# Rounding the low weight bits on ScalarE, fewer fill matmuls, and a later start of the scheduled loop

## The chip, the cores and the metric

The kernel runs on one core of one Trainium2 chip. The metric is the device time of one execution in microseconds, from a set of runs on the chip; beside it stands one execution that the hardware profiler recorded. A core has five engines, and each runs its own queue of instructions in order: PE (TensorE, matmuls), DVE (VectorE), ACT (ScalarE), POOL (GpSimd) and SP (SyncE, which here issues all DMAs). They wait for each other through semaphores.

## The reference

Three stages. An attention with a running state over 8 heads of 40, 768 tokens and a batch of 2; a first expert stage; a second one. Cut to what matters:

```python
m_new  = max(f + m, i);  f_s = exp(f + m - m_new);  i_s = exp(i - m_new)
C = f_s * C + i_s * outer(v, k);  n = f_s * n + i_s * k
y = sigmoid(o) * (C @ q) / max(|n . q|, 1)             # per head and token

h = max(x @ w1, x @ w2, x @ w3);  x = h @ w_out        # 320 -> 768 -> 320
h = x @ w_in;  g = h * tanh(log1p(exp(h)));  out = g @ w_out2   # 320 -> 2048 -> 320
```

The weights reach the chip as 64-bit floats, each as two 32-bit integer words (low, high).

## The kernel before, in words

**Tiles and stages.** Tokens come in 12 units of 128 (6 chunks of the sequence times 2 batches); blocks of 512 tokens (4 units) are what the expert stages work on. The matmuls run at a precision that takes each operand apart into a rounded high part and the rest (`xh` and `xl`, `w` with both, `hh` and `hl`), so one product is eight matmuls of 512 columns (`mm8`, line 340: five with `xh`, three with `xl`).

**A unit** runs through `spread` (line 139, tile `fp`: the decays on PE), `decay` (line 124, tile `dt`: two scans on DVE), `scores` (line 162, tiles `sc_0` and `sc_1`: keys times queries on PE, even heads from rows 0 to 63, odd heads from rows 64 to 127), `passed` (line 150, `cp`), `decayed` (line 167: `dt` times scores on DVE), `values` and `keys` on POOL (lines 173 and 184, `vp` and `kp`), `numer` (lines 204 and 206, tile `it`), `denom` (lines 212 to 214 on DVE, then line 216 `sg` times 1/den on POOL), `gated` (line 221 on DVE, tile `xn`; line 222 its pad on ACT), `transpose_x` (line 233 on PE, tile `xp`; line 235 the copy to `xh` on ACT), `lower_x` (`xl`), `outer` (line 256, `sp`) and `carry` (lines 268 and 270, the state `st`).

**A weight** is a tile of 128 x 640 numbers. `fetch` loads the raw words (`raw`, three buffers). `scaled` (line 285, ACT) takes the high word as a float times a power of two into `dec`. `merge` is three passes on DVE: line 292 shifts the low word right by 29 and sets its last bit (`low`), line 294 shifts `dec` left by 3 and ORs `low`, line 296 puts the sign bit back into `dec`. Then ACT (lines 307 to 309) rounds to the high part and POOL (lines 310 to 312) subtracts. There are 28 weights: nine `w` of the first expert stage, three plus eight `wo`, eight `wi`.

**What sets the order.** Lines 392 to 547 are one hand-written order on all engines: the setup, units 0 to 3 and the first product (`up(0, 0)`). In it `dummy` puts fill matmuls on PE whose result nobody reads (line 193, 128 x 512 from the tile `warm`, a part of `zraw`). The rest, from `follow(PLAN0)` on, gets its order from a scheduler at build time, which may put the loop's instructions between the hand-written ones once the last of some of them have gone out: line 581 names the five, on PE the `fence`, which is the last matmul of `outer(3)`. PLAN0 is `w2 a4 w3 u0.1 a5 w4 b4 w5 w6 b5 a6 w7 w8 a7 u0.2 b6 ...` (w a weight, a `attend`, b `finish`, u `up`).

Of the kernel before, what the change touches and what calls it, by code (L numbers as in the profile page):

```python
# [10 lines left out]
AF = mybir.ActivationFunctionType  # L11
ALU = mybir.AluOpType
PSUM = bass.MemoryType.PSUM

P = 128
B, H, S, D = 2, 8, 768, 40
# [20 lines left out]
BLOCKS = ((0, 512), (512, 512), (1024, 256), (1280, 256))  # L37
NU = NC * B
I32 = mybir.dt.int32


@with_exitstack
def mlstm_moe_kernel(ctx, tc, fi0, fir, qk2, q3, nat, w13, wo1, wi2, wo2, ident, bmask, out):
    nc = tc.nc
# [3 lines left out]
    stage = ctx.enter_context(tc.tile_pool(name="stage", bufs=1))  # L48
# [14 lines left out]
    def bank(tag, name):  # L63
        if tag == "mm":
            return mmp.tile([P, 512], F32, tag=tag, name=name)
        return pat.tile([P, 512], F32, tag=tag, bufs=3 if tag == "sm" else 1, name=name)
# [4 lines left out]
    idt = ac.tile([P, P + 2 * BH + 1], F32, tag="idt", name="idt")  # L71
# [42 lines left out]
    unit = {u: {} for u in range(NU)}  # L114
    warm = zraw[:, 0, 0:256].bitcast(mybir.dt.bfloat16)

    def heads(ap, e):
        return ap.rearrange("p (h e) -> p h e", h=H)
# [46 lines left out]
    def decayed(u, j):  # L165
        t = unit[u]
        nc.vector.tensor_tensor(t["dt"][:, j::2], t["sc"][j].rearrange("p (h t) -> p h t", h=4), t["dt"][:, j::2], op=ALU.mult)
# [18 lines left out]
    def gateo(u):  # L186
        sg = a2.tile([P, H, D], F32, tag="sg", name=f"sg{u}")
        nc.scalar.activation(sg, heads(loads[u][1][:, H * VD + DM:], D), AF.Sigmoid)
        unit[u]["sg"] = sg

    def dummy(ps, n):
        for _ in range(n):
            nc.tensor.matmul(ps, warm[:, 0:P], warm, start=True, stop=True)

    def numer(u, ps=None):
        c, b = u // B, u % B
        t = unit[u]
        ps = itbank(f"it{u}") if ps is None else ps
        it = heads(ps[:, 0:H * VD], VD)
        vt = vps[u % 2]  # L200
        for g in range(3):
            h1 = min(3 * g + 3, H)
            if c > 0:
                nc.tensor.matmul(it[:, 3 * g:h1], t["cb"][:, g], st[b][:, 3 * g:h1], start=True, stop=False)  # L204
            for h in range(3 * g, h1):
                nc.tensor.matmul(it[:, h], t["dt"][:, h], vt[:, h], start=(c == 0), stop=(c == 0 or h == h1 - 1))  # L206
        t["it"] = it

    def denom(u):
        num = unit[u]["it"]  # L210
        den = a2.tile([P, H, 1], F32, tag="den", name=f"den{u}")
        nc.vector.tensor_scalar(den, num[:, :, D:VD], -1.0, 1.0, op0=ALU.mult, op1=ALU.max)
        nc.vector.tensor_tensor(den, den, num[:, :, D:VD], op=ALU.max)
        nc.vector.reciprocal(den, den)
        sg = unit[u]["sg"]
        nc.gpsimd.tensor_tensor(sg, sg, den.to_broadcast([P, H, D]), op=ALU.mult)

    def gated(u):
        t = unit[u]
        xn = a2.tile([P, 3 * P], F32, tag="xn", name=f"xn{u}")  # L220
        nc.vector.tensor_tensor(heads(xn[:, 0:DM], D), t["it"][:, :, 0:D], t["sg"], op=ALU.mult)
        nc.scalar.activation(xn[:, DM:3 * P], xn[:, 2 * P:DM], AF.Copy)
        t["xn"] = xn

    def transpose_x(u, xp=None, fill=0):
        xh, xl = xs[u // 4]
        col = u % 4 * L
        xn = unit[u]["xn"]
        xp = bank("sm", f"xp{u}") if xp is None else xp
        dummy(xp, fill)  # L230
        xp = xp[:, 0:3 * L].rearrange("p (j t) -> p j t", j=3)
        for j in range(3):
            nc.tensor.transpose(xp[:, j], xn[:, j * P:(j + 1) * P], idt[:, 0:P])
        unit[u]["xp"] = xp
        return nc.scalar.activation(xh[:, :, col:col + L], xp, AF.Copy)  # L235

    def lower_x(u):
        xh, xl = xs[u // 4]
        col = u % 4 * L
        if u < B:  # L240
            xr = m1.tile([P, 3, L], F32, tag=f"hl{4 + u}", bufs=1, name=f"xr{u}")
            nc.scalar.activation(xr, unit[u]["xp"], AF.Copy)
            return lambda: nc.gpsimd.tensor_tensor(xl[:, :, col:col + L], xr, xh[:, :, col:col + L].bitcast(F32), op=ALU.subtract)
        if u >= 4:
            xr = a2.tile([P, 3, L], F32, tag="xr", bufs=1, name=f"xr{u}")
            nc.scalar.activation(xr, unit[u]["xp"], AF.Copy)
            return nc.gpsimd.tensor_tensor(xl[:, :, col:col + L], xr, xh[:, :, col:col + L].bitcast(F32), op=ALU.subtract)
        return nc.vector.tensor_tensor(xl[:, :, col:col + L], unit[u]["xp"], xh[:, :, col:col + L].bitcast(F32), op=ALU.subtract)

    def outer(u, sp=None, fill=0):  # L250
        sp = bank("sm", f"sp{u}") if sp is None else sp
        dummy(sp, fill)
        sp = sp[0:120, 0:9 * VD].rearrange("p (h e) -> p h e", h=9)
        kt, vt = kps[u % 2], vps[u % 2]
        for g in range(3):
            pe = nc.tensor.matmul(sp[:, 3 * g:3 * g + 3], kt[:, 3 * g:3 * g + 3].rearrange("p h e -> p (h e)"), vt[:, 3 * g:3 * g + 3], start=True, stop=True)  # L256
        unit[u]["sp"] = sp
        return pe
# [13 lines left out]
    raws = {}  # L272

    def fetch(src, name):
        raw = stage.tile([P, 640, 2], I32, tag="raw", bufs=RB, name=f"raw_{name}")
        raws[name] = raw
        return nc.sync.dma_start(raw, src)
# [3 lines left out]
    def scaled(src, name):  # L281
        if name not in raws:
            fetch(src, name)
        a = stage.tile([P, 640], F32, tag="dec", bufs=2, name=f"dec_{name}")
        nc.scalar.activation(a, raws[name][:, :, 1].bitcast(F32), AF.Copy, scale=2.0 ** -112)
        decs_[name] = a

    def merge(name):
        raw, a = raws.pop(name), decs_[name]
        lo, hi = raw[:, :, 0], raw[:, :, 1]  # L290
        t = stage.tile([P, 640], I32, tag="low", bufs=1, name=f"low_{name}")
        nc.vector.tensor_scalar(t, lo, 29, 1, op0=ALU.logical_shift_right, op1=ALU.bitwise_or)  # L292
        yield
        nc.vector.scalar_tensor_tensor(t, a.bitcast(I32), 3, t, op0=ALU.logical_shift_left, op1=ALU.bitwise_or)
        yield
        nc.vector.scalar_tensor_tensor(a.bitcast(I32), hi, -2147483648, t, op0=ALU.bitwise_and, op1=ALU.bitwise_or)

    def decode(src, name):
        scaled(src, name)
        for _ in merge(name):  # L300
            pass
        return decs_.pop(name)

    def split_lhs(z, w, eng):
        z = z.rearrange("p (s f) -> p s f", f=P)
        t = z[:, 4]
        nc.scalar.activation(w[:, 0:4], z[:, 0:4], AF.Copy)
        nc.scalar.activation(w[0:64, 8], t[0:64], AF.Copy)
        nc.scalar.activation(w[64:128, 9], t[64:128], AF.Copy)
        eng.tensor_tensor(w[:, 4:8], z[:, 0:4], w[:, 0:4].bitcast(F32), op=ALU.subtract)  # L310
        eng.tensor_tensor(w[64:128, 8], t[0:64], w[0:64, 8].bitcast(F32), op=ALU.subtract)
        return eng.tensor_tensor(w[0:64, 9], t[64:128], w[64:128, 9].bitcast(F32), op=ALU.subtract)
# [3 lines left out]
    def load_w13(g):  # L316
        name = f"w13_{g}"
        z = decs_.pop(name) if name in decs_ else decode(w13[g], name)
        w = wpool.tile([P, 10, P], F32R, tag=f"wa{g}", name=name)
        w1t[g] = w  # L320
        return split_lhs(z, w, nc.gpsimd)
# [70 lines left out]
    with tc.manual_schedule(engines={ET.PE, ET.DVE, ET.SP, ET.Activation, ET.Pool}):  # L392
# [7 lines left out]
        f, i = ft0[:, 0], ft0[:, 1]  # L400
# [84 lines left out]
        keys(2)  # L485
        nc.scalar.activation(gTr, gq[:, 0:NR * BH], AF.Copy)
        denom(1)
        carry(1)
        decayed(2, 0)
# [8 lines left out]
        mg = merge("w13_0")  # L498
# [13 lines left out]
        decayed(3, 0)  # L512
        queries(3)
        decayed(3, 1)
        transpose_x(1, bank("mm", "xp1"), 4)
        low1 = lower_x(1)
        denom(2)
        for _ in mg:
            pass
        next(mg, None)  # L520
        gateo(3)
        it3 = bank("sm", "it3")
        dummy(it3, 4)
        numer(3, it3)
        gated(2)
        denom(3)
        low1()
        scaled(w13[1], "w13_1")
        load_w13(0)
        mg = merge("w13_1")  # L530
        next(mg)
        outer(2, bank("mm", "sp2"))
        transpose_x(2, bank("mm", "xp2"), 4)
        next(mg)
        gated(3)
        for _ in mg:
            pass
        fsp = fetch(w13[3], "w13_3")
        fence = outer(3, bank("sm", "sp3"))
        lower_x(2)  # L540
        fact = transpose_x(3, bank("sm", "xp3"), 6)
        fetch(w13[2], "w13_2")
        fdve = lower_x(3)
        fpool = load_w13(1)
# [86 lines left out]
    low = {}  # L631
# [137 lines left out]
```

## Time and profile before

| | us |
|---|---|
| median of 3 runs | 403.36 (403.31 to 403.39) |
| the profiled execution | 404.21 |
| its span, first to last instruction | 402.4 |

The page of the profile gives the busy time of each engine over the span. A list of waits says for what an engine stood idle and how long. A table by window gives, for each stretch of the span, what each engine was busy, how many instructions it ran and which TensorE clock was granted (1.00 is the higher of its two levels, 2.4 GHz; 0.50 the lower, 1.2 GHz). A timeline gives instructions in order of time, runs of like ones in one line. Matmuls overlap their neighbours in these records, so the time of a group is read from its start to the start of what follows.

### The profile page before, as it was taken

What the parts mean: (1) busy time and instruction counts of PE and PEld (TensorE: products, weight loads), DVE (VectorE), ACT (ScalarE), POOL (GpSimd) and SP (SyncE); (2) the same over time, 40 slices, a digit from 0 to 9 for tenths busy, and PEclk for the clock granted to TensorE, in tenths of its full rate; (3) what the DMA queues carried; (4) which work ended last, traced back from release to release, by engine and by line L of the source; (5) the groups of instructions that cost most, each with busy time, mean ns of one, the idle gap of its engine ahead of it and who ended that gap; (6) DMA issues with size and microseconds to landing.
All of it is one profiled execution on the core that took longest, in us unless ns stands there. A gap on an engine that the chain in (4) does not pass through costs nothing.

```text
span 402.4 us, 6169 instructions
## 1 busy us (share of the span) xinstructions
PE 394.7 (98%) x2376; PEld 347.3 (86%) x2376; DVE 216.4 (54%) x340; ACT 173.2 (43%) x389; POOL 154.4 (38%) x155
## 2 busy tenths in 40 slices
PE   8999999999999999999999999999999999999996
PEld 5787887788888888888888889999898999999996
DVE  6897999678927277306823769962211221322220
ACT  3545655533543322256443586553332233434331
POOL 6666768934822223438851446651000010001000
PEclk9999999699999999999999999999999999999999
DMA  7696455632630012002320234300100000100100
GB/s 206 195 305 207 147 186 196 205 106 90 221 109 3 2 65 67 0 2 64 132 68 0 91 107 148 115 0 2 65 0 2 0 2 0 67 0 2 34 0 33
DMA packets 10410, 32.61 MB, mean 81 GB/s; under 512 B 1405, under 2 KB 4285, under 8 KB 10381
## 3 DMA queue, kind: packets, MB, share of 16 engines
q1 hardware_dynamic: 10381, 32.23, 24.8%
q8 instruction: 18, 0.29, 0.3%
q14 instruction: 11, 0.09, 0.1%
HBM read 30.26 MB, written 1.97 MB: 80 GB/s over the span
## 4 chain that ended last, share of the span: by engine, by line
PE 87%; DVE 6%; issue 3%; POOL 2%; ACT 1%; DMA 0%; DVEq 0%; POOLq 0%; ACTq 0%
PE h L340 22%; PE mm L340 21%; PE o L661 7%; PE o L663 7%; PE o L662 7%; PE it L206 4%; PE sc L162 3%; PE mz L371 2%; PE mz L372 2%; PE mz L373 2%; PE fp L139 2%; PE it L204 1%; DVE low_w L292 1%; PE sp L256 1%; DVE dt L124 1%
## 5 line engine op out<-in xcount | busy, mean ns | idle before, releaser
L645 DVE TENSOR_TENSOR gl<-g,gh 128x512 fp32r<-128x512 f32 (+1 forms) x64 | 38.3, 599 | 97.2 <-ACT g L644 97.2
L340 PE MATMUL mm<-xh,w 128*128 128x512 f32 x270 | 74.4, 403 | 0.6 <-ACT xh L235 0.6
L340 PE MATMUL h<-zh,wi 128*128 128x512 f32 (+1 forms) x320 | 67.7, 338 | 0.0
L643 ACT ACTIVATE gh<-h 128x512 fp32r<-128x512 f32 (+1 forms) x64 | 31.4, 491 | 83.6 <-PE h L340 77.6
L340 PEld LDWEIGHTS mm<-xh,w 128*128 128x128 f32 x270 | 50.4, 192 | 11.2 <-ACT xh L235 0.8
L663 PE MATMUL o<-wo,gl 128*128 128x320 f32 x192 | 59.4, 309 | 0.0
L662 PE MATMUL o<-wo,gh 128*128 128x320 f32 x192 | 59.3, 309 | 0.0
L661 PE MATMUL o<-wo,gh 128*128 128x320 f32 x192 | 59.2, 309 | 0.0
L340 PEld LDWEIGHTS h<-zh,wi 128*128 128x128 f32 x320 | 51.4, 189 | 4.7
L614 POOL TENSOR_TENSOR zl<-zraw,zh 128x512 fp32r<-128x512 f32 (+1 forms) x12 | 13.0, 1090 | 91.5 <-ACT zh L613 91.5
L340 PE MATMUL mm<-xl,w 128*128 128x512 f32 x162 | 47.8, 399 | 0.0
L340 PE MATMUL h<-zl,wi 128*128 128x512 f32 (+1 forms) x192 | 44.5, 338 | 0.0
L360 POOL TENSOR_TENSOR hl<-zraw,hh 128x512 fp32r<-128x512 f32 x18 | 25.4, 1411 | 47.6 <-ACT hh L359 47.4
L357 DVE TENSOR_TENSOR zraw<-zraw,mm 128x512 f32<-128x512 f32 x36 | 24.6, 682 | 33.6 <-PE mm L340 33.6
L661 PEld LDWEIGHTS o<-wo,gh 128*128 128x128 f32 x192 | 36.1, 188 | 1.3
L662 PEld LDWEIGHTS o<-wo,gh 128*128 128x128 f32 x192 | 36.1, 188 | 1.2
L340 PEld LDWEIGHTS mm<-xl,w 128*128 128x128 f32 x162 | 30.9, 191 | 6.8 <-issue 0.2
L663 PEld LDWEIGHTS o<-wo,gl 128*128 128x128 f32 x192 | 36.1, 188 | 0.0
L340 PEld LDWEIGHTS h<-zl,wi 128*128 128x128 f32 x192 | 31.8, 188 | 4.1
L644 ACT ACTIVATE g<-h 128x512 f32<-128x512 f32 (+1 forms) x64 | 31.2, 487 | 0.0
L124 DVE TENSOR_TENSOR_SCAN dt<-fp,idr 128x512 f32<-128x512 f32 x24 | 28.3, 1206 | 0.1
L206 PE MATMUL it<-vp,dt 128*128 128x41 f32 x192 | 25.2, 272 | 0.7 <-POOL vp L173 0.7
(138 smaller groups left out, 630.3 us busy)
## 6 DMA issues: line engine op xcount, KB each, us to landing
raw_wo<-in_wo_dram SPq DMA_DIRECT2D x11, 640.0 KB
na<-in_nat_dram SPq DMA_DIRECT2D x12, 484.0 KB
raw_w<-in_w_dram SPq DMA_DIRECT2D x9, 640.0 KB
raw_wi<-in_wi_dram SPq DMA_DIRECT2D x8, 640.0 KB
qall<-in_qk_dram SPq DMA_DIRECT2D x24, 160.0 KB
out_dram<-ob SPq DMA_DIRECT2D x12, 160.0 KB
q<-in_q_dram SPq DMA_DIRECT2D x10, 180.0 KB
idt<-in_ident_dram SPq DMA_DIRECT2D x1, 80.5 KB
```

Source lines behind the costliest of these rows:

```text
L124: nc.vector.tensor_tensor_scan(dtf[:, j * 512:(j + 1) * 512], unit[u]["fp"][j], idr, 0.0, op0=ALU.mult, op1=ALU.add)
L206: nc.tensor.matmul(it[:, h], t["dt"][:, h], vt[:, h], start=(c == 0), stop=(c == 0 or h == h1 - 1))
L340: nc.tensor.matmul(ps, a, r, start=(k == 0), stop=(k == 7))
L357: tops[blk, m] = nc.vector.tensor_tensor(top, top, pss[i], op=ALU.max)
L360: nc.gpsimd.tensor_tensor(ls, top, h.bitcast(F32), op=ALU.subtract)
L614: nc.gpsimd.tensor_tensor(zl[:, j], zv[:, j], zh[:, j].bitcast(F32), op=ALU.subtract)
L643: mark[blk, m] = nc.scalar.activation(gh, ps, AF.Mish)
L644: nc.scalar.activation(g, ps, AF.Mish)
L645: low[blk, m] = nc.vector.tensor_tensor(gl, g, gh.bitcast(F32), op=ALU.subtract)
L661: nc.tensor.matmul(po, a, whi, start=(m == 0), stop=False)
L662: nc.tensor.matmul(po, a, wlo, start=False, stop=False)
L663: nc.tensor.matmul(po, l, whi, start=False, stop=(m == KF2 - 1))
```

## The change

Four edits.

1. After line 285 `scaled` gets a second ACT pass, in place on the low words: taken as unsigned integers, times 15 * 2^-33, rounded to integers on writing back. In return `merge` loses its first DVE pass and the tile `low`; the two passes that are left read the low words in the raw buffer and work in `dec`.
2. The fills ahead of the transposes of units 1, 2 and 3 and of `numer(3)` go from 4, 4, 6 and 4 to one each.
3. In the hand-written order `low1` and `scaled(w13_1)` go out earlier, the last multiply of `denom(3)` goes from POOL to DVE, and `gated(3)` stands ahead of the merge of `w13_1`.
4. The `fence` on PE is the last transpose of unit 3 and no longer the last matmul of `outer(3)`.

```diff
@@ scaled, merge
         nc.scalar.activation(a, raws[name][:, :, 1].bitcast(F32), AF.Copy, scale=2.0 ** -112)
+        nc.scalar.activation(raws[name][:, :, 0], raws[name][:, :, 0].bitcast(U32), AF.Copy, scale=15 * 2.0 ** -33)
         decs_[name] = a
...
-        t = stage.tile([P, 640], I32, tag="low", bufs=1, name=f"low_{name}")
-        nc.vector.tensor_scalar(t, lo, 29, 1, op0=ALU.logical_shift_right, op1=ALU.bitwise_or)
-        yield
-        nc.vector.scalar_tensor_tensor(t, a.bitcast(I32), 3, t, op0=ALU.logical_shift_left, op1=ALU.bitwise_or)
+        b = a.bitcast(I32)
+        nc.vector.scalar_tensor_tensor(b, b, 3, lo, op0=ALU.logical_shift_left, op1=ALU.bitwise_or)
         yield
-        nc.vector.scalar_tensor_tensor(a.bitcast(I32), hi, -2147483648, t, op0=ALU.bitwise_and, op1=ALU.bitwise_or)
+        nc.vector.scalar_tensor_tensor(b, hi, -2147483648, b, op0=ALU.bitwise_and, op1=ALU.bitwise_or)
@@ denom
-    def denom(u):
+    def denom(u, eng=nc.gpsimd):
...
-        nc.gpsimd.tensor_tensor(sg, sg, den.to_broadcast([P, H, D]), op=ALU.mult)
+        eng.tensor_tensor(sg, sg, den.to_broadcast([P, H, D]), op=ALU.mult)
@@ the hand-written order
-        transpose_x(1, bank("mm", "xp1"), 4)
+        transpose_x(1, bank("mm", "xp1"), 1)
         low1 = lower_x(1)
         denom(2)
+        low1()
...
         gateo(3)
+        scaled(w13[1], "w13_1")
         it3 = bank("sm", "it3")
-        dummy(it3, 4)
+        dummy(it3, 1)
         numer(3, it3)
         gated(2)
-        denom(3)
-        low1()
-        scaled(w13[1], "w13_1")
         load_w13(0)
+        denom(3, nc.vector)
+        gated(3)
         mg = merge("w13_1")
+        outer(2, bank("mm", "sp2"))
+        transpose_x(2, bank("mm", "xp2"), 1)
         next(mg)
-        outer(2, bank("mm", "sp2"))
-        transpose_x(2, bank("mm", "xp2"), 4)
-        next(mg)
-        gated(3)
         for _ in mg:
             pass
         fsp = fetch(w13[3], "w13_3")
-        fence = outer(3, bank("sm", "sp3"))
+        outer(3, bank("sm", "sp3"))
         lower_x(2)
-        fact = transpose_x(3, bank("sm", "xp3"), 6)
+        fact = transpose_x(3, bank("sm", "xp3"), 1)
+        fence = unit[3]["pe"]
```

What the scheduler makes of it shows in the order of instructions. Line numbers of the changed kernel are one higher up to line 285, and the same again from line 294.

PE, from unit 3's `outer` to the first product's second part (`sp_487` and `sp_476` are unit 3's `sp`, `xp_492` and `xp_481` its transposes, `fp` and `cp` are those of unit 4; the fills ahead of the rows are left out), before:

```order
146 L139 MATMUL fp_0_581<-fzr,sel 128x128 x4
147 L139 MATMUL fp_1_586<-fzr,sel 128x128 x4
148 L233 MATMUL xp_492<-idt,xn_481 128x128 x2
149 L150 MATMUL cp_606<-fzr,sel_96 120x128 x3
150 L233 MATMUL xp_492<-idt,xn_481 128x128
151 L340 MATMUL mm_0_0_525<-xh_103,w_0_458 128x512 x5
```

and now:

```order
115 L257 MATMUL sp_476<-vp_92,kp_90 120x123 x3
116 L194 LDWEIGHTS zraw
117 L194 MATMUL xp_481<-zraw 128x512
118 L234 MATMUL xp_481<-idt,xn_459 128x128 x3
119 L140 MATMUL fp_0_564<-fzr,sel 128x128 x4
120 L140 MATMUL fp_1_569<-fzr,sel 128x128 x4
121 L151 MATMUL cp_589<-fzr,sel_96 120x128 x3
122 L340 MATMUL mm_0_0_509<-xh_103,w_0_447 128x512 x5
```

Unit 4's `fp` and `cp` went from between unit 3's transposes to behind them, ahead of the first product.

PE, unit 5 (`sc_0_688` and `sc_1_689`, now `sc_0_670` and `sc_1_671`), before:

```order
173 L162 MATMUL sc_0_688<-qall 128x128 x4
174 L204 MATMUL it_727<-st_98,cb_615 128x123
175 L206 MATMUL it_727<-vp_91,dt_591 128x41 x3
176 L204 MATMUL it_727<-st_98,cb_615 128x82
177 L206 MATMUL it_727<-vp_91,dt_591 128x41 x2
178 L340 MATMUL mm_2_0_953<-xh_103,w_3_626 128x512 x5
179 L340 MATMUL mm_2_0_953<-xl_104,w_3_626 128x512 x2
180 L162 MATMUL sc_1_689<-qall 128x128 x4
```

and now:

```order
144 L163 MATMUL sc_0_670<-qall 128x128 x2
145 L163 MATMUL sc_1_671<-qall 128x128 x2
146 L163 MATMUL sc_0_670<-qall 128x128
147 L163 MATMUL sc_1_671<-qall 128x128
148 L163 MATMUL sc_0_670<-qall 128x128
149 L163 MATMUL sc_1_671<-qall 128x128
```

The unit's two scans stand next to each other on DVE now (before, the merge of one weight, the first pass of the next and two maxima stood between them), and its even and odd heads stand together on PE. On PE that now holds for units 6 to 11 too; unit 4 still has its four even heads ahead of its four odd ones.

DVE, between the scans of unit 4 and the first product's second part (`st_98` is the carry of unit 2, `w_2` the third weight), before:

```order
59 L124 SCALAR_TENSOR_TENSOR dt_591<-fp_0_581,idr 128x512
60 L124 SCALAR_TENSOR_TENSOR dt_591<-fp_1_586,idr 128x512
61 L270 SCALAR_TENSOR_TENSOR st_98<-sp_467,bmt,st_98 120x3x41 x2
62 L270 SCALAR_TENSOR_TENSOR st_98<-sp_467,bmt,st_98 120x2x41
```

and now:

```order
57 L125 SCALAR_TENSOR_TENSOR dt_574<-fp_0_564,idr 128x512
58 L125 SCALAR_TENSOR_TENSOR dt_574<-fp_1_569,idr 128x512
59 L294 SCALAR_TENSOR_TENSOR dec_w_2_544<-dec_w_2_544,raw_w_2_487 128x640
60 L296 SCALAR_TENSOR_TENSOR dec_w_2_544<-raw_w_2_487,dec_w_2_544 128x640
61 L271 SCALAR_TENSOR_TENSOR st_98<-sp_462,bmt,st_98 120x3x41 x2
62 L271 SCALAR_TENSOR_TENSOR st_98<-sp_462,bmt,st_98 120x2x41
```

The third weight's merge went ahead of the carry of unit 2, whose bank (`sp`) the third part of the first product (`mm_0_2`) takes over.

## Rows read from the trace of the kernel before

**Rows 1.** The page: busy time of an engine, share of the span, instructions.
```profile
PE 394.7 (98%) x2376; PEld 347.3 (86%) x2376; DVE 216.4 (54%) x340; ACT 173.2 (43%) x389; POOL 154.4 (38%) x155
```

**Rows 2.** What PE waited for: in total us, times, the longest.
```profile
PE sc L162 <- DVE dt L124: 1.5, 2, 0.8
```

**Rows 3.** PE's timeline, 64 to 74 us: start, length, instructions, idle before.
```profile
66.95 0.71 PE L162 MATMUL sc<-qall 64*128 64x128 f32 x4 [0.79 <-DVE dt L124]
...
71.83 2.07 PE L162 MATMUL sc<-qall 64*128 64x128 f32 x12 [0.67 <-DVE dt L124]
```

**Rows 4.** Stretches of the span: length, busy time of each engine, granted clock.
```profile
12.00:28.00 16.00, 15.13 (x137) 13.71 (x138) 15.26 (x25) 7.32 (x18) 9.99 (x12) 1.00 0.76 236
...
38.00:72.00 34.00, 32.29 (x189) 26.98 (x190) 33.63 (x49) 20.80 (x54) 25.38 (x28) 1.00 0.53 171
...
66.20:71.80 5.60, 4.21 (x35) 3.97 (x35) 5.57 (x9) 3.31 (x8) 3.94 (x5) 1.00 0.37 117
...
71.90:78.70 6.80, 6.80 (x24) 5.51 (x25) 4.63 (x11) 4.13 (x11) 6.57 (x7) 0.50 0.63 205
```

**Rows 5.** The core: its span and mean granted clock.
```profile
core 0: 402.4 us, clock 0.992
```

**Rows 6.** PE's timeline, 27 to 40 us, columns as in rows 3.
```profile
27.61 1.03 PE L193 MATMUL xp<-zraw 128*128 128x512 bf16 x4
28.48 0.49 PE L233 MATMUL xp<-idt,xn 128*128 128x128 f32 x3
...
34.59 1.46 PE L193 MATMUL xp<-zraw 128*128 128x512 bf16 x6
35.69 1.19 PE L139 MATMUL fp<-fzr,sel 128*128 128x128 f32 x8
...
38.11 1.42 PE L340 MATMUL mm<-xh,w 128*128 128x512 f32 x5 [0.58 <-ACT xh L235]
```

**Rows 7.** DVE's timeline, 27 to 46 us: ahead of the transposes, and two carries.
```profile
28.86 0.44 DVE L292 TENSOR_SCALAR low_w<-raw_w 128x640 int32<-128x640 int32 x1
...
31.34 0.48 DVE L221 TENSOR_TENSOR xn<-it,sg 128x320 f32<-128x320 f32 x1
...
34.40 0.48 DVE L221 TENSOR_TENSOR xn<-it,sg 128x320 f32<-128x320 f32 x1
...
41.21 1.50 DVE L270 SCALAR_TENSOR_TENSOR st<-sp,bmt,st 120x123 f32<-120x123 f32 x6
```

**Rows 8.** POOL's timeline, 27 to 45 us: what stands ahead of the first weight.
```profile
33.76 1.59 POOL L243 TENSOR_TENSOR xl<-xr,xh 128x384 fp32r<-128x384 f32 x1
35.29 1.88 POOL L310 TENSOR_TENSOR w<-dec_w,w 128x512 fp32r<-128x512 f32 x1
```

**Rows 9.** PE's score matmuls alone (line 162), in eight stretches for units 4 to 11.
```profile
42.00:47.00 5.00, 1.97 (x16) 1.00 0.39 128
53.00:60.00 7.00, 2.31 (x16) 1.00 0.56 187
66.00:74.00 8.00, 2.77 (x16) 0.87 0.45 159
85.00:87.00 2.00, 1.17 (x16) 1.00 0.00 0
...
sum 39.00, PE 14.44; mean PE 1.80
```

**Rows 10.** Line 292 on DVE alone, 38 to 72 us.
```profile
38.00:72.00 34.00, 5.74 (x7) 1.00 0.53 171
```

**Rows 11.** Line 285 on ACT alone, 38 to 72 us.
```profile
38.00:72.00 34.00, 5.51 (x7) 1.00 0.53 171
```

**Rows 12.** POOL's timeline, 70 to 82 us: unit 5's gate behind a weight.
```profile
77.64 1.28 POOL L310 TENSOR_TENSOR w<-dec_w,w 128x512 fp32r<-128x512 f32 x1
...
80.08 0.72 POOL L216 TENSOR_TENSOR sg<-sg,den 128x320 f32<-128x320 f32 x1
```

**Rows 13.** DVE's timeline, 62 to 85 us: what waits for that gate.
```profile
80.84 0.49 DVE L221 TENSOR_TENSOR xn<-it,sg 128x320 f32<-128x320 f32 x1 [2.01 <-POOL sg L216]
```

More of the change, by code (lines that the diff above doesn't have):

```diff
@@ L39 @@
 I32 = mybir.dt.int32
+U32 = mybir.dt.uint32
 @with_exitstack
@@ L232, in transpose_x @@
         for j in range(3):
-            nc.tensor.transpose(xp[:, j], xn[:, j * P:(j + 1) * P], idt[:, 0:P])
+            unit[u]["pe"] = nc.tensor.transpose(xp[:, j], xn[:, j * P:(j + 1) * P], idt[:, 0:P])
         unit[u]["xp"] = xp
```

## The prediction

> **What bounds the kernel now.** The page first: PE is busy for 394.7 of 402.4 us, DVE for 216, ACT for 173, POOL for 154 [rows 1]. So only what PE runs, what PE waits for, and PE's clock can shorten the kernel by much; DVE counts only where PE stands behind it. The list of PE's waits gives that place: of what the change can reach, the longest is `sc` behind the scan `dt` on DVE, 1.5 us in two pieces [rows 2], at 66.95 and 71.83 us [rows 3]. The table by windows says why: from 38 to 72 us DVE is busy for 33.63 of 34.00 us, while ACT has 13.2 us free and POOL 8.6 [rows 4]. There, and almost nowhere else, DVE is the bound. The clock comes last: its mean is 0.992 [rows 5], which over 402.4 us is 3.2 us of full clock that were not granted, and one stretch holds it all: 71.9 to 78.7 us at 0.50, the lower level, with PE busy throughout [rows 4]. At the higher level those 6.8 us would be 3.4. Ahead of it PE was busy for 4.21 of 5.60 us and in small matmuls only [rows 4], with the two waits in it. From 12 to 28 us PE also runs small matmuls, but is busy for 15.13 of 16.00 us and keeps 1.00 [rows 4]. So I read the half clock as what the two waits behind DVE brought about: they cost 1.5 us themselves and 3.4 us behind them.
>
> **The change, part by part.** The sum is made against the profiled execution, 404.21 us; the median of the runs is 403.36, so 0.85 comes off at the end.
>
> *Fills.* 14 of 18 are removed. Four took 0.87 us from start to the next start (27.61 to 28.48), six took 1.10 (34.59 to 35.69) [rows 6], so one is 0.18 to 0.22 and 14 are 2.6 to 3.0; I take 0.21 and 2.9. The idle 0.58 us ahead of the first product, until the copy of unit 3 to `xh` is done [rows 6], goes as well: unit 4's `fp` and `cp` now lie behind unit 3's transposes and fill the time of that copy, at no cost, because they are work that has to be done anyway. If they didn't cover it, 0.6 would come back. But the fills stood over waits. What must now come earlier too is `xn` of units 2 and 3 on DVE, at 31.34 and 34.40 us [rows 7], and the first weight's subtraction on POOL, which began at 35.29 behind `low1` of 1.59 us, and took 1.88 [rows 8]. For `xn` of unit 2 only line 292's 0.44 us goes away ahead of it [rows 7], while PE arrives 1.9 us earlier (nine fills at 0.21): the slack that the fills gave is used up, and PE waits for 0 to 0.5 us. `xn` of unit 3 is better off: its gate no longer waits for POOL and two merge passes no longer stand ahead of it. On POOL `low1` goes out about 3 us earlier and frees the weight in time, but not by much. Together 0.3 to 1.2 us are given back; I take 0.8, the short chain of unit 2 and a wait of the first `xl` product for `low` of unit 3. Sum: -2.9 - 0.6 + 0.8 = -2.7.
>
> *Score matmuls.* Even heads use rows 0 to 63, odd heads 64 to 127. Where both kinds alternate, 16 records take 1.17 us (unit 7); where four of a kind stand apart, 2.31 (unit 5) [rows 9]. The eight units take 14.44 us together; of that unit 6's 2.77 holds about 1.0 that is half clock (its second piece, 2.07 us [rows 3], at half clock), which is counted below, so 13.4. In the new order units 5 to 11 alternate: 7 * 1.17 = 8.2, and unit 4 lies between today's 1.97 and unit 5's 2.31 [rows 9]. That is 10.2 to 10.5, a gain of 2.9 to 3.2. Every group also overlaps its neighbours by about 0.1 (27.61 + 1.03 reaches past 28.48 by 0.16 [rows 6]), and there are five fewer groups: 0.3 to 0.6 is no gain. I take -2.6.
>
> *DVE loses line 292, ACT gets a pass.* Between 38 and 72 us line 292 took 5.74 us in seven instructions, 0.82 each [rows 10], almost twice the 0.44 of an undisturbed one [rows 7]. DVE's 33.63 us becomes 27.9 of 34. The two waits for `dt`, 0.79 and 0.67 us [rows 3], go: -1.5. On ACT nothing in this trace reads integers, rounds and writes them in place. The nearest row is line 285, the same 128 x 640 words at the same stride: 5.51 us for seven, 0.79 each [rows 11]. As bounds I take the cheapest and the dearest pass of the decoding in these rows, on whichever engine: 0.44 on DVE [rows 7] and 1.88 on POOL [rows 8]. I take 0.79, since engine, reading and shape are the same: seven are 5.5, and ACT is then busy for 26.3 of 34 us, under DVE's load; hidden beside PE. Should it be 1.88, ACT is full (34.0 of 34) and the gain here is gone. The scheduler puts the new pass ahead of the old one of the preceding weight, so ACT can stand at words that haven't landed with the splits of finished weights queued behind; I give that nothing, as each fetch now starts earlier by what DVE saves.
>
> The Trainium skill says the opposite of this edit: the page "ScalarE: Activation LUTs", section "Rules for kernel authors", advises VectorE rather than ScalarE for plain multiplies and the like, as the faster engine for each element. By an undisturbed row it is right, 0.44 on DVE [rows 7] against 0.79 on ACT [rows 11]; by that alone the 28 passes would be a loss of 28 * 0.35 = 9.8 us of engine time. The trace decides by load and not by price: DVE is full in that stretch and ACT is not [rows 4].
>
> *Clock.* With the two waits gone, the stretch at 0.50 should not come: -3.4.
>
> *New waits.* Three, all from the new order. The bank of the third product (`mm_0_2`) is that of unit 2's `sp`, which the carry on DVE frees; a weight's merge of two passes now stands ahead of that carry, whose row is six instructions for 1.50 us at 41.21 [rows 7]: PE's two products before it need some 2.5 us, so 0 to 1.2; I take 0.7. Unit 5's gate on POOL still stands behind the last weight's subtraction (77.64, the gate at 80.08) [rows 12], and DVE waited 2.01 us for it then [rows 13], with PE busy on products at half clock. PE now gets through those products in half the time, and arrives earlier: a wait for unit 5's `xn` of 0.5 to 2; I take 1.4. The scans of unit 7 behind it on DVE give 0 to 1, I take 0.7. Together +2.8 (0.5 to 4.2).
>
> **Sum.** -2.7 - 2.6 - 1.5 - 3.4 + 2.8 = -7.4: 396.8 for the profiled execution, and 396.0 for the median.
>
> **The rivals.**
>
> *The half clock comes back.* 14 fills are gone from a stretch of small matmuls with waits in it, and the new wait of 1.4 us at unit 5's `xn` is as long as the two old ones together; both resemble what stood ahead of 71.9 us, where 25% of PE's time was idle [rows 4]. For it: my own new waits add up to some 1.3 us in the 8 us before the first product. Against it: after unit 5's `xn` come long products within little time, and the stretch from 12 to 28 us, small matmuls with 5% idle, kept the clock. One such stretch costs what it does now, 3.4 us: 399.4. The Trainium skill has such a rule, on the page "TensorE: Matmul & The Clock Gate", section "A second HAM failure mode: psum-queue depth-cycling": frequent short idle times between groups of matmuls make the clock fall and rise again. This trace agrees in one place, 71.9 us, and the fills that are removed are what would guard against it.
>
> *ACT becomes the bound, and the kernel is slower.* Place: 38 to 80 us, the nine weights of the first expert stage. Price: if the integer pass costs much more than line 285. ACT has 13.2 us free from 38 to 72 [rows 4], seven passes fill that at 1.9 us each, and above it every further 0.1 us costs 0.7 us on the way to the weights that PE waits for. The 2.7 of the fills and the 2.6 of the scores stay, the waits and the half clock come back, and the sum is slower from about 2.7 us a pass; at 3 us a pass about 406. For it: no row shows such a pass. Against it: ACT's time in this trace goes by elements, and these are the same in number.
>
> *The scheduled waits don't come.* If POOL's gate of unit 5 moves up with DVE, the new waits are 0.5 and not 2.8: 393.7.
>
> *The edit does nothing for PE.* If the two passes left on DVE get slower by what line 292 took, because the low words now come at a stride from the raw buffer, the waits of 1.5 and the half clock stay. Then only fills and scores count, -5.3 less the carry's 0.7: about 398.8 in the median. Line 296 reads the raw words at that stride already, so I give it little.
>
> **How the numbers follow.** The forecast 0.50 (394.4 to 397.8 with the bounds of waits and fills); half clock back 0.31 (398 to 400.5); ACT the bound 0.07, of which 0.05 end slower and 0.01 about equal; waits absent 0.06; nothing for PE 0.06. The range takes in the first two and most of the last two: 393.8 to 400.5, with some 0.15 left out. A measurement of this kernel can tell 0.2%, 0.8 us, from no change. Faster 0.92, same 0.03, slower 0.05.
>
> **What would show it.** Right: the first product at 35 us and not 38.11; the list of PE's waits without `sc` behind `dt` at units 5 and 6, and with `xp` behind `xn` near 76 us; a mean clock of 1.00; score groups of units 5 to 11 at 1.17; the new ACT line at 0.8; DVE well under full from 38 to 72 us. Wrong: a stretch at 0.50 in the windows (rival one, by 3.4 us), the new line over 1.9 us or PE waiting for `w` (rival two), lines 294 and 296 longer than before.

## The result and the profile after

The changed kernel took 398.39 us in the median (397.92 to 404.23, six executions) against 403.38 before; the ratio is 0.988 with an interval of 0.9866 to 0.9895. The forecast was 396.0 within 393.8 to 400.5, so faster, by 5.0 where 7.4 was expected. One sentence is needed to read the numbers below: in some executions PE's clock falls between 11 and 16 us, in instructions that the change doesn't touch (six of the fourteen profiles show it, neither of the two of the kernel before does), and the time is then up to 13 us longer, so times below stand with their mean clock where it matters, and the profile shown is of an execution without that (the run `again_2` below, the changed kernel once more, 398.57 us, clock 0.995).

PE's waits in it, in us in total, times, the longest:

```profile
PE xp L234 <- ACT hh L359: 2.1, 1, 2.1
...
PE mm L340 <- DVE st L271: 1.1, 1, 1.1
PE xp L234 <- ACT xn L223: 0.8, 1, 0.8
...
PE mm L340 <- DVE xl L249: 0.2, 1, 0.2
```

The two waits for `dt` [rows 2] and the idle time ahead of the first product [rows 6] are gone; three new ones of 0.8 us or more are there, and two short ones (0.2 for `xl`, and 0.4 at 197 us). Where they stand, in PE's timeline (start, length, instructions, idle before):

```profile
34.69 1.37 PE L340 MATMUL mm<-xh,w 128*128 128x512 f32 x5
...
42.02 1.40 PE L340 MATMUL mm<-xh,w 128*128 128x512 f32 x5 [1.09 <-DVE st L271]
...
64.50 0.33 PE L234 MATMUL xp<-idt,xn 128*128 128x128 f32 x1 [0.83 <-ACT xn L223]
...
78.73 0.85 PE L234 MATMUL xp<-idt,xn 128*128 128x128 f32 x3 [2.06 <-ACT hh L359]
```

The first product starts 3.4 us earlier than at 38.11 [rows 6]. The last row is unit 5's transposes: the list names `hh` on ACT as the releaser, but `xn` on DVE ended in the same moment, at 78.58 us, and both stood behind POOL, which the chain below shows. The stretches that answer rows 4 (length, busy time of PE, PE's loads, DVE, ACT and POOL, granted clock):

```profile
38.00:72.00 34.00, 32.08 (x207) 27.52 (x206) 30.60 (x49) 27.31 (x65) 26.66 (x29) 1.00 0.56 182
...
76.00:79.00 3.00, 0.94 (x5) 0.51 (x5) 0.91 (x2) 1.69 (x4) 2.16 (x5) 0.96 0.17 65
79.00:82.50 3.50, 3.50 (x26) 3.38 (x26) 3.50 (x7) 1.75 (x6) 2.55 (x4) 0.55 0.00 0
```

DVE is no longer full, ACT is at 27.3 of 34, and the half clock is back behind unit 5's wait, but shorter: 3.5 us at a mean of 0.55 lose 1.6. The integer pass on ACT (minimum, median and maximum in ns), and the score matmuls of units 4 to 11 that answer rows 9:

```profile
L287 ACT ACTIVATE raw_w<-raw_w x9: 761/800/833, 24.4 to 62.8; 128x640 int32<-128x640 uint32 x9
```

```profile
sum 117.00, PE 10.28; mean PE 1.29
```

Against 14.44 before, of which about 1.0 was half clock (here 0.4, in unit 7).

**The ledger**, from the profile before (404.21 us) to this one (398.57, so -5.64): first product -3.42; wait for `xl` +0.17, for the carry +1.09, for unit 4's `xn` +0.83, for unit 5's +2.06, for a copy at 197 us +0.45; the two waits for `dt` -1.46; half clock -3.4 and +1.6; scores 10.28 - 0.4 of half clock against 13.4, less 0.5 for five groups that no longer overlap a neighbour, -3.0. That is -5.1. It closes to 0.6 us for these two executions; what each item was worth by itself is another matter, as the experiments show.

### The profile page after: what moved, and what is told of

It reads as the page before. It is cut to its first block, busy times and chain, and to the rows that moved or that the text cites. A ratio compares the mean times of both kernels' runs of the same rounds, so it can differ in the third digit from the quotient of the medians.

```text
span 402.3 us, 6093 instructions
## 1 busy us (share of the span) xinstructions
PE 392.5 (98%) x2362; PEld 346.8 (86%) x2362; DVE 195.4 (49%) x313; ACT 191.7 (48%) x417; POOL 149.5 (37%) x154
## 4 chain that ended last, share of the span: by engine, by line
PE 76%; ACT 7%; DMA 5%; POOL 5%; DVE 4%; issue 2%; SPq 0%; POOLq 0%; ACTq 0%; DVEq 0%
PE h L340 21%; PE mm L340 15%; PE o L663 7%; PE o L662 7%; PE o L661 7%; PE it L207 4%; DMA raw_w<-in_w_dram 3%; PE sc L163 2%; PE mz L371 2%; PE mz L372 2%; PE mz L373 2%; DMA qall<-in_qk_dram 2%; PE fp L140 2%; PE sp L257 1%; PE it L205 1%
## 5 line engine op out<-in xcount | busy, mean ns | idle before, releaser
L207 PEld LDWEIGHTS it<-vp,dt 128*128 128x128 f32 x192 | 26.5, 206 | 0.9 <-issue 0.6
```

## The experiments

Each kernel ran beside the kernel before on the same chip. An edit also means another order by the scheduler, which is told where it decides.

**The changed kernel twice more.** No edit.

> The changed kernel once more, for a profile with no disturbed start. Theory one (the half clock came back behind the new wait for unit 5's xn): median 397.9, mean clock 0.995; the windows show one stretch at 0.50 after the wait of xp near 76 us, and nowhere else. Rival (the clock is lost somewhere else, in the part without fills before 36 us): the wait near 76 us has the clock at 1.00 behind it, and the stretch at 0.50 lies before 40 us.

> The changed kernel, a third time, for a profile at a mean clock of 1.00 or 0.995. Theory one: 397.2 to 398.0 us; first product near 35 us, PE waits for st 0.7 to 1.2, for xp 1.5 to 2.0, for xl 0.2. Rival: what one execution at 1.00 showed (397.2) is not the kernel's usual time, and 397.9 with a short stretch at 0.50 behind the wait of xp is.

The first gave 397.17 at a clock of 1.00 and five executions of 400.7 to 410.3 with clocks of 0.966 to 0.986, so its median of 405.38 lies above the 403.35 of the kernel before beside it. In its profile (410.26 us) the clock went before anything that was changed, after PE's waits for unit 1's `qall`:

```profile
10.68 0.49 PE L163 MATMUL sc<-qall 64*128 64x128 f32 x2 [1.28 <-DMA qall<-in_qk_dram]
11.97 2.07 PE L163 MATMUL sc<-qall 64*128 64x128 f32 x14 [0.80 <-DMA qall<-in_qk_dram]
```

The second gave 397.52 to 400.76 and the profile shown above, in which PE also waited for that tile, 0.76 us, and kept its clock. The profiles disagree on the two theories. In `again` it is the rival's picture: the half clock lies before 40 us (11.7 to 39.0), and PE's wait of 1.95 us at unit 5 has the clock at 1.00 behind it. In `again_2`, and in the profile of the first run, the half clock stands behind unit 5's wait, as theory one has it (3.4 and 6.8 us long). Whether the changed kernel is more liable to the early fall stays open: its clock was under 0.99 in 8 of its 16 executions, that of the kernel before in 7 of the 70 with a clock on record. But the instructions up to 24 us are the same, and none of the 20 executions of the four variants below that keep edits 1 to 3 was under 0.99.

**The kernel before once more.** No edit.

> The kernel before, once more, for a second profile. The profile that the prediction used had 6.8 us at 0.50 and took 404.21; other executions had a mean clock of 1.00 and took 403.2 to 403.4. Theory one: the half clock cost only that difference, about 0.9, since at the full clock PE would stand and wait there: with a mean clock of 1.00 the wait of xp behind unit 5's xn, absent before, shows near 76 to 80 us with 1.5 to 2.5 us. Rival (the prediction's): half clock costs half its length, 3.4 us; then an execution at 1.00 takes 400.8 and shows no new wait.

403.26 to 405.28 in ten; six with a clock of 1.00 took 403.30 to 403.85. The profile is of an execution of 403.26 us with the half clock cut short (columns as above):

```profile
72.00:74.00 2.00, 2.00 (x13) 1.76 (x12) 2.00 (x5) 1.26 (x4) 1.92 (x2) 0.51 0.67 268
74.00:76.00 2.00, 2.00 (x7) 1.54 (x6) 1.88 (x6) 1.65 (x4) 1.85 (x4) 0.64 0.35 77
```

That is a loss of 1.7 us of clock and not the 3.4 of rows 4, and still the execution is no slower than those at 1.00, and only 0.95 faster than the profile of before. The reason is two engines further on. POOL and then DVE in this execution:

```profile
77.55 1.29 POOL L310 TENSOR_TENSOR w<-dec_w,w 128x512 fp32r<-128x512 f32 x1
...
79.98 0.72 POOL L216 TENSOR_TENSOR sg<-sg,den 128x320 f32<-128x320 f32 x1
```

```profile
80.74 0.49 DVE L221 TENSOR_TENSOR xn<-it,sg 128x320 f32<-128x320 f32 x1 [3.01 <-POOL sg L216]
81.15 0.68 DVE L357 TENSOR_TENSOR zraw<-zraw,mm 128x512 f32<-128x512 f32 x1
81.74 2.33 DVE L124 TENSOR_TENSOR_SCAN dt<-fp,idr 128x512 f32<-128x512 f32 x2
```

And PE, whose transposes of unit 5 came at 83.75 and whose 16 scores of unit 7 took 1.17 us in the profile of before [rows 9]:

```profile
82.05 0.38 PE L233 MATMUL xp<-idt,xn 128*128 128x128 f32 x2
...
83.37 1.91 PE L162 MATMUL sc<-qall 64*128 64x128 f32 x16
```

Unit 5's gate is at 79.98 here and at 80.08 in rows 12, whatever PE's clock does: POOL, not PE, sets when unit 5's `xn` and behind it unit 7's scans and scores can come. PE reaches unit 5's transposes 1.7 us earlier, and 0.7 of that is lost again at unit 7's scores, which take 1.91 us because the scans ahead of them end at 84.07. Theory one holds for the price, about 0.9 at most. The wait for `xn` that it expects at a clock of 1.00 wasn't seen, since no profile is of such an execution.

**The score matmuls by themselves.** The kernel before, where from unit 4 on the scheduler must keep the matmuls of a unit in their written order:

```diff
         for h in range(H):
             r = 64 * (h % 2)
+            with ExitStack() as es:
+                if banks is None and h > 0 and u >= 4:
+                    es.enter_context(tc.issue_after(mm.ins))
-            nc.tensor.matmul(scs[h % 2][:, (h // 2) * L:(h // 2 + 1) * L], qk[r:r + 64, 1, h // 2], qk[r:r + 64, 0, h // 2], start=True, stop=True)
+                mm = nc.tensor.matmul(scs[h % 2][:, (h // 2) * L:(h // 2 + 1) * L], qk[r:r + 64, 1, h // 2], qk[r:r + 64, 0, h // 2], start=True, stop=True)
```

> The kernel before with one thing added: from unit 4 on, the scheduler must give the score matmuls in the order even, odd, even, odd. No other edit. It measures the term of the scores by itself. By the prediction -2.6 of it, less unit 7 and 11, which alternate already: 400.5 to 401.5. Rival (in the part before unit 5's xn PE waits behind POOL's gate anyway, so only units 8, 9 and 10 count, 0.3 to 0.9 us each): 401.8 to 402.6. Third: the order forced on PE costs as much in waits as it gains, 403.4.

Ratio 1.0007 (0.9971 to 1.0043): no gain is shown. The two fastest took 402.70 and 402.85, at clocks of 0.995 and 0.998. The scores of the eight units did get shorter, though most were still cut in two by other matmuls:

```profile
sum 115.00, PE 12.23; mean PE 1.53
```

13.4 to 12.2 by the records, and 0.5 us of time at best, between the rival and the third. The saving is all in units 4 to 6 (about 6.0 to 4.4); units 7 to 11 went from 7.4 to 7.8, so what shorter scores behind unit 5 are worth wasn't measured. Nor is the rival's reason shown here: unit 5's gate stood at 79.36 us, but PE came to its transposes only at 82.97, without a wait. What the record does show is new waits ahead of that, 0.62 for unit 4's `xn` and 0.43 for `dt`.

**Low bits on ACT, alone.** The kernel before with edit 1 of the change and nothing else, but for one step of the merge less in the hand-written order:

```diff
         mg = merge("w13_1")
-        next(mg)
```

> The kernel before with the low bits made on ACT and nothing else (fills, fence and the order of units 1 to 3 as before, two merge passes). By the prediction it gains the two waits of sc behind dt (1.5) and part of the scores: 400 to 402. Rival (POOL's chain to unit 5's gate sets the end of that part, so less on DVE gives PE a wait at xp in their place): 402.5 to 403.5, with a wait of xp of 1 to 2 us in the list.

399.75 to 400.95 in the four executions at a clock of 1.00: -2.4 to -3.5, ratio 0.9951 (0.9923 to 0.9978). DVE is no longer full from 38 to 72 us (30.45 of 34), though one wait for `dt` of 0.83 us is left. PE found another wait, behind ACT, whose queue stood at words that hadn't landed:

```profile
77.27 0.78 ACT L287 ACTIVATE raw_wo<-raw_wo 128x640 int32<-128x640 uint32 x1 [0.76 <-DMA raw_wo<-in_wo_dram]
77.95 0.57 ACT L355 ACTIVATE zraw<-mm 128x512 f32<-128x512 f32 x1
```

```profile
78.58 1.83 PE L340 MATMUL mm<-xh,w 128*128 128x512 f32 x5 [1.45 <-ACT zraw L355]
```

**Few fills, alone.** The kernel before with edit 2 and nothing else:

```diff
-        transpose_x(1, bank("mm", "xp1"), 4)
+        transpose_x(1, bank("mm", "xp1"), 1)
...
-        dummy(it3, 4)
+        dummy(it3, 1)
...
-        transpose_x(2, bank("mm", "xp2"), 4)
+        transpose_x(2, bank("mm", "xp2"), 1)
...
-        fact = transpose_x(3, bank("sm", "xp3"), 6)
+        fact = transpose_x(3, bank("sm", "xp3"), 1)
```

> The kernel before with one fill each in place of 4, 4, 4 and 6, and nothing else. By the prediction's first step 14 fills are worth 2.9 less 0.8 of waits: 400.5 to 401.5. Rival (the fills stand over waits for xn and the first weight, which the other edits of the change shorten): the first product starts less than 1.5 us earlier, waits of xp behind xn appear near 31 to 35 us, 402 to 403.4.

400.54 to 401.89, ratio 0.9934 (0.9908 to 0.996). The first product is earlier by 2.3, and its `xh` and weight are late:

```profile
35.79 0.73 PE L340 MATMUL mm<-xh,w 128*128 128x512 f32 x2 [0.58 <-ACT xh L235]
37.19 0.96 PE L340 MATMUL mm<-xh,w 128*128 128x512 f32 x3 [0.67 <-POOL w L311]
```

So the fills are worth 1.4 to 2.8, near the prediction's 2.1; the rest of the 3.4 is about the size of these two waits, which the changed kernel doesn't have. DVE is as full as before in this kernel (33.59 of 34.00 from 38 to 72 us), and unit 5's gate came at 79.94 although PE started 2.3 us earlier: PE waited 1.71 us for unit 5's transposes instead.

**The changed kernel with one edit undone**, three times: the low bits back on DVE (the ACT pass out, the merge of before in its place), the fills of before (the last diff turned round), and the fence of before:

```diff
-        outer(3, bank("sm", "sp3"))
+        fence = outer(3, bank("sm", "sp3"))
...
-        fence = unit[3]["pe"]
```

> The changed kernel with the low bits made on DVE again (the three passes of before), edits 2 to 4 kept. By the prediction the ACT pass is worth DVE's two waits for dt (1.5 us) and the half clock behind them (3.4): 400 to 402 us, PE waiting for sc or st behind DVE between 40 and 70 us. Rival (the fills, the fence and the order made the gain, the ACT pass none): 397.5 to 398.5.

> The changed kernel with the fills of before (4, 4, 4 and 6), all else as changed. By the prediction 14 fills less are worth 2.9 less 0.8 of uncovered waits, and the scheduler's order of the scores changes with it (units 5, 8 and 9 in fours, up to 3 us more): 400 to 403. Rival (the fills only stood over waits): 397.5 to 398.5. If the fills also guard the clock, the mean clock is above 0.995 and the time is lower by up to 2 us than the first figure.

> The changed kernel with the fence of before (the last matmul of outer(3)), so that unit 4's fp and cp may go between unit 3's transposes again. The prediction gave the later fence 0.6 us (the idle ahead of the first product). Theory one: 0.5 to 1 us for that, and the scheduler's order has units 5, 8 and 9 in fours again, 1 to 3 us: 399 to 401. Rival (unit 4 starts earlier and DVE's scans with it, which helps more than the idle costs): under 398.

Low bits on DVE: 402.44 to 406.91 at clocks of 0.983 to 0.996, above the 400 to 402 expected and no faster than the kernel before (ratio 1.0022, 0.9988 to 1.0056), though part of that is clock. PE waits for `xn` on DVE, at units 2, 3 and 5, and not for `sc` or `st`:

```profile
33.96 0.68 PE L234 MATMUL xp<-idt,xn 128*128 128x128 f32 x3 [0.71 <-DVE xn L222]
37.04 0.68 PE L234 MATMUL xp<-idt,xn 128*128 128x128 f32 x3 [1.55 <-DVE xn L222]
...
85.01 0.44 PE L234 MATMUL xp<-idt,xn 128*128 128x128 f32 x2 [1.98 <-DVE xn L222]
```

Without the pass on ACT the shorter start turns into waits for DVE. Fills back: the six executions at 0.998 or more took 400.79 to 402.38, some 3 to 5 above 397.2 to 397.5, as predicted, and PE waits only 0.2 us for unit 5's `xn`, since PE comes there later. But the scheduler's order changed with it, and the scores are longer than in the kernel before:

```profile
sum 117.00, PE 14.83; mean PE 1.85
```

So these 3 to 5 us are not the fills alone. Six of ten kept their clock, against one of six of the changed kernel beside them; whether that is the fills, the shorter wait at unit 5 or the start isn't separated. Old fence: 400.92 to 401.35. The 0.58 us of idle time is back (first product at 35.05, 0.36 later than 34.69), but that doesn't explain some 3 us. The scores are:

```profile
sum 117.00, PE 15.40; mean PE 1.92
```

10.28 to 15.40, about 0.6 of it half clock: from 54 to 61 us the clock is at 0.50 to 0.52, behind a wait for `dt` of only 0.40 us. By these records the fence is worth far more by what it does to the scheduler's order than by what it does to the start.

**Unit 5's gate.** The changed kernel with it on DVE, then on POOL ahead of one weight, then ahead of two weights with the scores held in order. The first, in `finish(u)`:

```diff
-        denom(u)
+        denom(u, nc.vector if u == 5 else nc.gpsimd)
```

The second and the third, in `load_w13(g)` (LATEW is (8,) and (7, 8); `gate` is the multiply of `denom`):

```diff
+        if g in LATEW:
+            with tc.issue_after(unit[5]["gate"].ins):
+                return split_lhs(z, w, nc.gpsimd)
         return split_lhs(z, w, nc.gpsimd)
```

> The changed kernel with unit 5's gate multiply (line 217) on DVE in place of POOL, so that it no longer stands behind the last weight's subtraction. Theory one: the wait of xp (1.4 to 1.9 us) and the half clock behind it (2.0 us by the mean clock of 0.995) both go: 394.0 to 395.0, clock 1.00. Rival (the clock is lost elsewhere): only the wait goes, 396.0 to 396.5, clock 0.995. Third: DVE was needed elsewhere in that stretch and the wait moves to dt or st: 397.5 to 398.5.

> The changed kernel with POOL's order at one place turned round: unit 5's gate multiply ahead of the last weight's three subtractions, the gate still on POOL. With the gate on DVE the time was 399.6 and not 394 to 395, but the order of all else moved with it, and the multiply took 1.61 us there. Theory one (the gate behind the weight costs PE the wait of xp): wait of xp down from 1.9 to under 0.5, 395.5 to 396.5. Rival (ACT's queue holds the chain just as late, the pad of xn or the copies): the wait stays over 1 us, 397.2 to 398.5. Third: the scheduler's other order gives scores in fours or splits and eats it, 398 to 400.

> The changed kernel with unit 5's gate on POOL ahead of the subtractions of the last two weights, and the scores held to even, odd, even, odd. Gate ahead of one weight moved the gate from 77.3 to 75.5 us and the time by 0.3 to 0.8. Theory one (POOL's order sets unit 5's xn): the gate near 73 to 74 us, the wait of xp under 0.7 and no stretch at 0.50 behind it, 395.0 to 396.5. Rival (the next in line, unit 7's scans or the weights that POOL now gives later, takes it): the wait moves to sc behind dt or to mm behind w, 396.7 to 398.

On DVE: 399.23 to 401.03, four at 1.00 from 399.23 to 400.02, slower than any of the three expectations. The clock came back and the time didn't: the multiply takes 1.61 us beside a busy POOL, ACT's pad of `xn` comes late, and PE waits twice all the same; units 8 to 11 have their scores apart (12.87 us in all).

```profile
70.47 1.61 DVE L217 TENSOR_TENSOR sg<-sg,den 128x320 f32<-128x320 f32 x1
```

```profile
72.76 0.41 PE L234 MATMUL xp<-idt,xn 128*128 128x128 f32 x2 [0.44 <-DVE xn L222]
...
75.11 0.33 PE L234 MATMUL xp<-idt,xn 128*128 128x128 f32 x1 [1.52 <-ACT xn L223]
```

Ahead of one weight: 396.69 (clock 1.00) to 398.13, against 397.52 to 400.76 of the changed kernel on the same chip. The gate moves from 77.33 to 75.51 us and the wait from 2.06 to 1.55:

```profile
75.51 0.72 POOL L218 TENSOR_TENSOR sg<-sg,den 128x320 f32<-128x320 f32 x1
```

The gate moved by 1.8, but units 9 and 11 have their scores apart and the gain is 0.4 to 0.8; it is the fastest version here, though four executions on one chip don't separate it for certain. The wait and the time are the rival's, the place isn't: PE stood behind `xn` on DVE, which the gate released. Ahead of two weights: the gate is at 71.78 us, `xn` on DVE at 72.55, in good time, and PE waits longer than ever, because ACT has the pad of `xn` behind words that are not there:

```profile
74.96 0.79 ACT L291 ACTIVATE raw_wo<-raw_wo 128x640 int32<-128x640 uint32 x1 [2.03 <-DMA raw_wo<-in_wo_dram]
75.65 0.24 ACT L227 ACTIVATE xn<-xn 128x64 f32<-128x64 f32 x1
```

```profile
75.95 0.33 PE L238 MATMUL xp<-idt,xn 128*128 128x128 f32 x1 [2.35 <-ACT xn L227]
```

397.61 to 399.87, no faster than the changed kernel. The rival had the place wrong, but the sign right: a next one in line took it, and it is ACT's queue.

## Why the prediction held, and where it didn't

**What bounds the kernel**: right in the main. With one pass less on DVE and one more on ACT alone, 2.4 to 3.5 us went. The chain of work that ended last, followed back through the stretch from 38 to 72 us, has some two thirds of its time on DVE in the kernel before, and no load ("issue" is time in which the engine waited for nothing that the profile shows):

```profile
by line: issue 30.0%; DVE low_w L292 15.9%; DVE dt L124 14.7%; DVE low_w L294 10.5%; DVE zraw L357 8.3%; DVE dec_w L296 7.0%; DVE st L270 4.3%; DVE dt L167 4.1%; DVE cb L178 1.8%; PE sc L162 1.7%; ACT xh L235 1.5%; DVE xn L221 1.3%; DVE den
```

In the changed kernel loads of the raw words and ACT's pass over them take half of it:

```profile
by line: DMA raw_w<-in_w_dram 41.6%; issue 8.8%; ACT raw_w L287 8.6%; DVE dt L125 6.7%; ACT st L269 5.1%; ACT dec_w L286 4.4%; POOL vp L174 3.9%; POOL w L310 3.7%; POOL hl L360 3.2%; POOL w L312 2.7%; DVE dec_w L294 2.5%; DVE dec_w L296 2.5
```

That DVE was the only bound isn't shown: with few fills alone it was as full, and the kernel was 1.4 to 2.8 us faster.

**Fills and fence** (-2.7): -3.4 at the first product. The waits given back were sized too high at `xn` of units 2 and 3 (0.1 each and less); whether the later fence or DVE's gate of unit 3 saved them isn't separated, as edit 3 never ran by itself.

**Scores** (-2.6): -3.0 by the records of the whole change; alone, 1.2 less busy time gave 0.5 at best. The step that failed is to count busy time of PE as path. In the kernel before and its three variants above, unit 5's gate came between 79.36 and 80.21 us whatever PE did ahead of it, and in the changed kernel PE waits 2.06 us there: of what PE saves ahead of that place, part turns into waiting.

**The ACT pass** (0.79 us, ACT at 26.3): 0.80 and 27.3, right. By the rule that the prediction weighed against it (the Trainium skill, page "ScalarE: Activation LUTs", section "Rules for kernel authors": VectorE for plain multiplies) the move alone would be a loss; measured, it is the gain of 2.4 to 3.5 us above, and the measurement decides. DVE came to 30.6 and not 27.9: other work moved into the stretch (49 instructions, as before), and the last merge pass, now seven times there and not six, took 1.29 us on average and not 1.16. The sentence "I give that nothing", on ACT standing at words that haven't landed, was wrong. PE waits 0.83 us for it at unit 4 of the changed kernel, and it stopped three of the experiments (1.45, 1.52 in part, 2.35). The chain at unit 4, on ACT:

```profile
62.83 0.80 ACT L287 ACTIVATE raw_w<-raw_w 128x640 int32<-128x640 uint32 x1 [1.07 <-DMA raw_w<-in_w_dram]
63.54 0.76 ACT L286 ACTIVATE dec_w<-raw_w 128x640 f32<-128x640 f32 x1
64.21 0.24 ACT L223 ACTIVATE xn<-xn 128x64 f32<-128x64 f32 x1
```

**Clock** (-3.4): the term that was mis-sized most. The half clock before was worth some 0.9 us at most, as executions with half or all of it gone show; the prediction took half its length off and then added waits at the same place (1.4 and 0.7) as another term, where both are one thing: slack behind POOL's gate. The 0.85 that came off at the end counts it again, since the executions of the median take the 403.3 us of those at a clock of 1.00. Nor do the runs bear out that the waits bring the half clock about: 0.40 us in the kernel with the old fence had 6.8 us of it behind it, 1.95 us in `again` none.

**New waits** (+2.8): carry 1.09 (0.7 taken; the two products ahead of it took 4.2 us, from 34.69 to 38.87, and not the 2.5 of the prediction, but the carry came later still, at 41.08), unit 5's `xn` 2.06 (1.4), unit 7's scans nothing on PE (0.7), unit 4's `xn` 0.83 (not seen). The sum is 4.0 and carries, with the 1.6 of half clock behind it, the 2 us between forecast and result. That the result lies in the range is in part luck: a clock term and a score term that were too large stood against waits that were too small. Rival one, the half clock's return, is true in small; ACT full by a dear pass is not (27.3 of 34, 0.80 us); the other two are not.

What sets unit 5's `xn` in the changed kernel is POOL, which has no gap from 67.73 us to the gate:

```profile
67.73 1.82 POOL L360 TENSOR_TENSOR hl<-zraw,hh 128x512 fp32r<-128x512 f32 x1 [3.20 <-ACT hh L359]
...
77.33 0.72 POOL L217 TENSOR_TENSOR sg<-sg,den 128x320 f32<-128x320 f32 x1
```

```profile
78.09 0.49 DVE L222 TENSOR_TENSOR xn<-it,sg 128x320 f32<-128x320 f32 x1 [4.09 <-POOL sg L217]
```

It was idle for 3.20 us ahead of that, in order behind `hh`. The chain that ended last goes on from there, back to the load of a weight's raw words (start, length, what; most pieces left out):

```profile
56.42 6.33 DMA raw_w<-in_w_dram
...
62.83 0.80 ACT raw_w L287
...
66.96 0.64 ACT hh L359
...
67.73 1.10 POOL hl L360
...
77.29 0.78 ACT dec_wo L286
...
78.73 0.85 PE xp L234 x3
```

By this chain unit 4's wait and unit 5's have one origin, words that landed at 62.75 us, and POOL's order is only the last part of the way. Open: the integer pass held behind the landing of its words on ACT, or behind the copies and pads that PE waits for, wasn't tried; neither was an earlier load, a weight on POOL in that gap, or edit 3 by itself.

## What to carry to other kernels

Take time off an engine's busy sum only where that engine sets the end; here a gain of PE that was counted in full (the half clock, and part of the scores) lay ahead of a gate on POOL that came at 80 us whatever PE did. When a pass moves to an engine with room, ask not only whether it fits but what stands behind it in that queue when its input is late: a pass over freshly loaded words on ACT held up copies or pads that PE waited for in five of the kernels here. And where a scheduler sets the order, the same edit is worth 0.4 or 3 us by what it does to that order, so a single edit undone is no measure of the edit by itself.

## What the runs showed of the hardware

A multiply of 128 x 320 on DVE took 0.49 us when it started with POOL idle (unit 3's gate in the changed kernel) and 1.61 with POOL at work (unit 5's gate on DVE, above); the last merge pass took 0.81 with POOL idle and, beside a long subtraction on POOL from 39.09 us on, 1.78:

```profile
31.95 0.49 DVE L217 TENSOR_TENSOR sg<-sg,den 128x320 f32<-128x320 f32 x1
...
39.38 1.78 DVE L296 SCALAR_TENSOR_TENSOR dec_w<-raw_w,dec_w 128x640 int32<-128x640 int32 x1
...
66.84 0.81 DVE L296 SCALAR_TENSOR_TENSOR dec_w<-raw_w,dec_w 128x640 int32<-128x640 int32 x1
```

The Trainium skill, page "SBUF — State Buffer", section "SBUF: two separate sides", has a rule for it: an instruction of VectorE with two inputs in SBUF and one of GpSimd that reads SBUF take a shared pair of ports, whole instruction by whole instruction, and the later one stands. The rows agree. Line 292, the pass that the change takes off DVE, took 0.44 us undisturbed and 0.82 on average from 38 to 72 us [rows 7, 10]; that POOL is the reason there isn't shown.

An integer pass on ACT, read as unsigned, scaled, rounded and written back in place at a stride, took 0.80 us in the median, against 0.79 for the float pass of that shape (line 286) in the same profile.
